# A fused sketch-attention and FFN kernel rewritten: residual algebra, block transposes, column tiles, a scheduled order

## The chip, the cores and the metric

The kernel runs on one core of one Trainium2 chip. Times are device microseconds (us) from launch to end on that core; a run here means one timed execution. Ratios of two kernels are the mean time of one kernel's fast runs over the mean time of the other's fast runs of the same rounds, so they are not quite the ratio of the medians quoted beside them. All comparisons are between runs of state fast, except where a slow one is named.

Engines: PE is the matmul engine (TensorE), DVE the vector engine, ACT the scalar engine (tanh and copies), POOL a second vector engine that is hardly used here, SP the queue that issues most DMAs.

## The reference, cut to what matters

```python
B, H, S, D, r = 4, 4, 1088, 32, 8         # q, k, v: (B, H, S, D) float32; S1, S2: (r, D)
def phi(x):                               # 64 features: outer product of two 8-vectors
    a = S1 @ x;  b = S2 @ x
    return outer(a, b)
kv  = sum_s phi(k_s) v_s^T                # 64 x 32 per batch and head
z   = sum_s phi(k_s)
att = (phi(q) @ kv) / (phi(q) @ z + 1e-6)
x   = att with heads side by side         # (4352, 128)
h   = x @ w_in                            # 128 -> 2048
out = (h - tanh(h)) @ w_out               # 2048 -> 128
```

Two facts of this algebra are used below. First, `(h - tanh(h)) @ w_out = x @ (w_in @ w_out) - tanh(h) @ w_out`. Second, the denominator `phi(q) @ z` is a bilinear form in `S1 q` and `S2 q`, so it can be had from an 8 by 8 matrix per head instead of from a 64-long feature vector.

## The kernel before

Tokens lie on partitions. A chunk of 128 tokens of one batch is transposed on PE, projected, multiplied out, transposed again, and so on. This is the query half of a chunk (waits and buffers cut):

```python
def B_step(b_, c_, qwait, kvzwait):
    tensor.transpose(psT, q_bt[:, c_])                    # token-major -> feature-major
    scalar.copy(T_sb, psT)
    tensor.matmul(psAB, T_sb, psbd)                       # S1 q, S2 q for four heads (float32)
    scalar.copy(ab_sb, psAB)
    vector.tensor_tensor(qp_sb, a[..., None], b[:, None]) # outer product, 256 columns
    for hp in range(2): tensor.transpose(bank_q, qp_sb)   # 2 x 128x128
    scalar.copy(qpT_sb, bank_q)
    for hp in range(2): tensor.matmul(psND, qpT_sb, kvzp_sb)   # numerator and denominator
    vector.tensor_scalar(dtmp, den, 1e-6, add)
    vector.reciprocal(rden, dtmp)
    vector.tensor_tensor(xrow, num, rden, mult)
    tensor.transpose(psX, xrow)                           # back to feature-major for the FFN
    scalar.copy(xT_sb, psX)                               # -> bf16
```

The key half (`A_step`) has the first five steps; after nine chunks of a batch `KVZ` runs 18 float32 matmuls (36 records in the trace). The FFN is cut into blocks that are pulled, about two at a time, after each attention step:

```python
def block_task(jb):                                       # 16 per group of up to 512 tokens
    tensor.matmul(psH, w_in_sb[:, jb*128:(jb+1)*128], xtoks)       # waits for the bank: mF
    scalar.activation(t_sb, psH, Tanh)
    vector.tensor_tensor(g_sb[:, jb], psH, t_sb, subtract)         # frees the bank
def layer2_mm_task():
    for jb in range(16): tensor.matmul(psO, w_out_sb[:, jb], g_sb[:, jb], accumulate)
    ...   # copy, four PE transposes back to token-major, four copies, one DMA
```

There are eight PSUM banks (the buffers that matmuls write): three for attention steps, two for query transposes, three in a ring for the FFN. 1088 tokens are padded to nine chunks of 128.

## Time and profile before

| | before |
|---|---|
| time, median of 4 runs | 471.05 us (469.07 to 473.68) |
| traced span | 470.1 us |
| PE busy, ACT busy, DVE busy | 306.1, 158.2, 150.2 us |
| mean granted PE clock in the trace | 0.665 |
| first tanh starts at | 63.4 us |

The first fence is the page of the profile: busy time of each engine (share of the span, number of instructions), two rows of its 40 equal slices (busy tenths of PE, granted PE clock in tenths), and the chain of waits followed back from the last instruction, by engine and by line.

```profile
PE 306.1 (65%) x1032; PEld 171.8 (37%) x1032; DVE 150.2 (32%) x372; ACT 158.2 (34%) x476; POOL 11.9 (3%) x23
...
PE   0585566677665756686666665685567767778674
...
PEclk9999999996555665555555755755555655665965
...
PE 54%; ACT 20%; DVE 14%; issue 8%; POOL 2%; DMA 1%; ACTq 0%; POOLq 0%
PE psm L536 26%; PE psst L536 23%; ACT tanh L536 8%; DVE g L536 5%; PE psq L536 5%; ACT Tsb L536 4%; DVE qp L536 3%; ACT qpT L536 3%; DVE xrow L536 2%; ACT absb L536 2%; DVE rden L536 1%; DVE dtmp L536 1%; ACT hb L536 1%; POOL psbd L536 1%;
```

No engine is near full, and the chain changes hands all the time. The trace in order of time shows why. This is one query chunk; columns are start, duration, engine, operation and tiles, and in brackets how long the engine had been idle and what ended the wait.

```profile
108.72 0.42 DVE L536 TENSOR_TENSOR qp<-absb 128x256 f32<-128x256 f32 x1 [0.82 <-ACT absb L536]
...
109.20 0.44 PE L536 MATMUL psq<-ident,qp 128*128 128x128 f32 x2 [0.76 <-DVE qp L536]
109.67 0.37 ACT L536 COPY qpT<-psq 128x256 f32<-128x256 f32 x1 [0.99 <-PE psq L536]
...
110.10 0.89 PE L536 MATMUL psst<-kvzp,qpT 128*128 128x66 f32 x4 [0.46 <-ACT qpT L536]
111.02 0.16 DVE L536 TENSOR_SCALAR dtmp<-psst 128x4 f32<-128x4 f32 x1 [1.88 <-PE psst L536]
111.22 0.18 DVE L536 RECIPROCAL rden<-dtmp 128x4 f32<-128x4 f32 x1
111.43 0.29 DVE L536 TENSOR_TENSOR xrow<-psst,rden 128x128 f32<-128x128 f32 x1
...
111.78 0.47 PE L536 MATMUL psst<-ident,xrow 128*128 128x128 f32 x1 [0.79 <-DVE xrow L536]
...
112.29 0.27 ACT L536 CAST xT<-psst 128x128 bf16<-128x128 f32 x1 [2.25 <-PE psst L536]
...
112.33 7.92 PE L536 MATMUL psm<-vbt,wbt 128*128 128x66 f32 x36
```

Each step starts when the one before it ends, on another engine. From one numerator to the next it is 7 to 10 us in 26 of the 35 steps from chunk to chunk, and 11.5 to 17.7 us in the other nine. The last line is the float32 kv chain of the batch.

The second half of the story is PE's clock. The next fence is the listing by windows: the stretch, its length, then busy us (and number of instructions) of PE, weight loads, DVE, ACT, POOL, then the granted clock, the DMA share and GB/s.

```profile
core 0: us, PE busy (x) PEld busy (x) DVE busy (x) ACT busy (x) POOL busy (x), PEclk, DMA share, GB/s
114.00:116.00 2.00, 2.00 (x12) 2.00 (x11) 0.00 (x0) 0.00 (x0) 0.00 (x0) 0.50 0.89 177
...
432.00:434.00 2.00, 2.00 (x6) 0.73 (x5) 0.00 (x0) 0.00 (x0) 0.00 (x0) 0.50 0.00 0
434.00:436.00 2.00, 2.00 (x9) 0.81 (x8) 0.00 (x0) 0.00 (x0) 0.00 (x0) 0.84 0.00 0
...
442.00:444.00 2.00, 1.33 (x4) 0.29 (x3) 2.00 (x4) 1.97 (x4) 0.00 (x0) 1.00 0.00 0
446.00:448.00 2.00, 1.79 (x3) 0.29 (x3) 1.96 (x4) 1.79 (x3) 0.00 (x0) 0.50 0.00 0
```

At 431.3 us sixteen w_out matmuls begin back to back. 3.4 us later the clock goes from 0.50 to 1.00. All eight rises in this trace fall in such a chain, 2.6 to 6.0 us after its start. While FFN blocks are then paced by DVE (one 512-column matmul per 0.60 us), the clock stays up to 445 us and falls back. The kv chain at 112.3 us is dense in the record, and the clock stays at 0.50 (window 114 to 116). So PE runs at half clock most of the time; whether its waits are the reason is tested below (before_nl1_warm). The clock row of the page shows 9 in its first slices, but the trace has no clock record before 103.6 us; the kv matmuls of batch 0 at 26.6 us take the same 7.92 us as those at 112.3 us, where the record says 0.50. The mean of 0.665 counts that stretch as full; at 0.50 there it would be about 0.55, an estimate.

### The profile page before, as it was taken

The numbers are of one execution on the slowest core, as the hardware profiler recorded it, in microseconds if no ns is written. First come the engines' busy times: TensorE is split into PE (matmuls) and PEld (weight loads), VectorE is DVE, ScalarE is ACT, GpSimd is POOL, SyncE is SP. The second block draws the span as 40 slices with busy tenths as digits, with TensorE's granted clock in tenths as the row PEclk, the third lists the DMA queues.
The fourth block names the chain that finished last, engine by engine and source line by source line (L and its number), as shares of the span: only waits on it lengthen the run. The fifth ranks groups of instructions, "written<-read, shape, count | busy, mean of one in ns | idle before, by whom it ended". The sixth has DMA issues, their size and how long they took to land.

```text
span 470.1 us, 3569 instructions
## 1 busy us (share of the span) xinstructions
PE 306.1 (65%) x1032; PEld 171.8 (37%) x1032; DVE 150.2 (32%) x372; ACT 158.2 (34%) x476; POOL 11.9 (3%) x23
## 2 busy tenths in 40 slices
PE   0585566677665756686666665685567767778674
PEld 0373333336433334474332332373432232231222
DVE  0211233411245223211453155103244235256623
ACT  2412233411244223212342344113234225355733
POOL 9100000000000000000000000000000000000000
PEclk9999999996555665555555755755555655665965
DMA  7760000002400024002000300030000000000000
GB/s 203 111 102 2 0 0 1 0 0 53 71 1 1 0 51 64 1 1 42 12 0 0 61 5 0 1 57 1 0 15 0 0 25 1 0 27 0 22 0 26
DMA packets 59443, 11.26 MB, mean 24 GB/s; under 512 B 54432, under 2 KB 58784, under 8 KB 59296
## 3 DMA queue, kind: packets, MB, share of 16 engines
q1 hardware_dynamic: 58496, 8.92, 10.9%
q10 hardware_dynamic: 672, 2.10, 1.4%
q8 instruction: 9, 0.15, 0.1%
q0 software_dynamic: 256, 0.01, 0.1%
q14 instruction: 10, 0.08, 0.1%
HBM read 8.79 MB, written 2.23 MB: 23 GB/s over the span
## 4 chain that ended last, share of the span: by engine, by line
PE 54%; ACT 20%; DVE 14%; issue 8%; POOL 2%; DMA 1%; ACTq 0%; POOLq 0%
PE psm L536 26%; PE psst L536 23%; ACT tanh L536 8%; DVE g L536 5%; PE psq L536 5%; ACT Tsb L536 4%; DVE qp L536 3%; ACT qpT L536 3%; DVE xrow L536 2%; ACT absb L536 2%; DVE rden L536 1%; DVE dtmp L536 1%; ACT hb L536 1%; POOL psbd L536 1%; ACT outsb L536 1%
## 5 line engine op out<-in xcount | busy, mean ns | idle before, releaser
L536 DVE TENSOR_TENSOR g<-psm,tanh 128x512 bf16<-128x512 f32 (+1 forms) x192 | 97.2, 553 | 84.0 <-ACT tanh L536 82.1
L536 ACT ACTIVATE tanh<-psm 128x512 bf16<-128x512 f32 (+1 forms) x192 | 85.9, 491 | 16.4 <-PE psm L536 15.8
L536 PE MATMUL psm<-xT,w_in 128*128 128x512 bf16 (+1 forms) x192 | 81.5, 499 | 13.2 <-DVE g L536 12.3
L536 PE MATMUL psst<-psbd,Tsb 128*128 128x64 f32 x144 | 47.7, 433 | 42.4 <-ACT Tsb L536 39.4
L536 PEld LDWEIGHTS psst<-psbd,Tsb 128*128 128x128 f32 x144 | 34.6, 298 | 73.6 <-ACT Tsb L536 70.4
L536 PE MATMUL psm<-g,w_out 128*128 128x512 bf16 (+1 forms) x192 | 53.5, 463 | 11.4 <-DVE g L536 9.8
L536 PE MATMUL psst<-kvzp,qpT 128*128 128x66 f32 x144 | 38.8, 422 | 16.7 <-ACT qpT L536 16.7
L536 DVE TENSOR_TENSOR wbt<-absb 128x256 f32<-128x256 f32 x36 | 15.3, 425 | 90.0 <-ACT absb L536 90.0
L536 PEld LDWEIGHTS psm<-xT,w_in 128*128 128x128 bf16 x192 | 26.7, 145 | 45.8 <-DVE g L536 36.9
L536 PEld LDWEIGHTS psst<-kvzp,qpT 128*128 128x128 f32 x144 | 32.0, 309 | 30.5 <-ACT qpT L536 30.5
L536 PE MATMUL psq<-ident,qp 128*128 128x128 f32 x72 | 23.8, 432 | 27.5 <-DVE qp L536 27.5
L536 ACT CAST xT<-psst 128x128 bf16<-128x128 f32 x36 | 9.6, 266 | 87.7 <-PE psst L536 87.7
L536 PEld LDWEIGHTS psm<-g,w_out 128*128 128x128 bf16 x192 | 22.9, 136 | 41.4 <-issue 34.7
L536 PE MATMUL psst<-ident,xrow 128*128 128x128 f32 x36 | 17.1, 474 | 28.6 <-DVE xrow L536 28.6
L536 ACT COPY absb<-psst 128x64 f32<-128x64 f32 x72 | 15.3, 213 | 55.3 <-PE psst L536 55.3
L536 DVE TENSOR_TENSOR qp<-absb 128x256 f32<-128x256 f32 x36 | 15.3, 425 | 54.0 <-ACT absb L536 54.0
L536 PE MATMUL psm<-vbt,wbt 128*128 128x66 f32 x144 | 31.6, 422 | 1.0 <-issue 0.9
L536 DVE TENSOR_SCALAR dtmp<-psst 128x4 f32<-128x4 f32 x36 | 5.8, 162 | 82.6 <-PE psst L536 82.6
L536 PEld LDWEIGHTS psm<-vbt,wbt 128*128 128x128 f32 x144 | 31.0, 332 | 1.6 <-issue 1.3
L536 ACT COPY qpT<-psq 128x256 f32<-128x256 f32 x36 | 13.4, 372 | 43.7 <-PE psq L536 43.7
L536 ACT COPY hb<-psm 128x512 f32<-128x512 f32 (+1 forms) x12 | 5.8, 480 | 59.3 <-PE psm L536 59.3
L536 PE MATMUL psst<-ident,kbt 128*128 128x128 f32 x36 | 14.9, 415 | 11.6 <-DMA kbt<-in_k_dram 11.6
(28 smaller groups left out, 129.1 us busy)
## 6 DMA issues: line engine op xcount, KB each, us to landing
kbt<-in_k_dram SPq DMA_DIRECT2D x32, 64.0 KB, 2.5
vbt<-in_v_dram SPq DMA_DIRECT2D x32, 64.0 KB, 2.5
qbt<-in_q_dram SPq DMA_DIRECT2D x32, 64.0 KB, 2.4
out_dram<-outsb SPq DMA_DIRECT2D x8, 256.0 KB, 2.4
w_in_f<-in_moe_w_in_dram ACTq DMA_DIRECT2D x1, 1024.0 KB, 5.1
psbd<-in_S_dram POOLq DMA_DIRECT2D x8, 1.0 KB, 2.6
kbt<-in_k_dram SPq DMA_DIRECT2D x4, 32.0 KB, 2.3
vbt<-in_v_dram SPq DMA_DIRECT2D x4, 32.0 KB, 2.3
```

Source lines behind the costliest of these rows:

```text
L536: ins = getattr(eng_obj, od.method)(*od.args, **od.kw)
```

## The change

The intent is to take work off the token-major path and off DVE, and to make every engine's order overlap-friendly. Five things change together.

```diff
-op("vector", "tensor_tensor", out=g_sb[gs][:, jb, 0:T], in0=psH, in1=t_sb[hs][:, 0:T], op=ALU.subtract)
-... 16 matmuls of g_sb with w_out_sb
+P.add("scalar", ... e.activation(out=th.ap, in_=hv.ap, func=AF.Tanh, scale=-1.0))        # -tanh(h)
+seq = [("t", j) for j in range(NJB)]
+seq[8:8] = [("c", wch), ("c", wcl)]      # x @ (w_in @ w_out), as bf16 high part and bf16 low part
+... 18 matmuls into one bank; w_in @ w_out itself: 16 transposes and 16 matmuls, once
```

```diff
-op("tensor", "transpose", out=psT, in_=k_bt[slot][:, c_, :, :], identity=ident)   # per 128 tokens
-op("scalar", "copy", T_sb[p], psT)
+src = k[b].rearrange("h (t c) d -> (h t) (c d)", c=NC)       # 34 blocks of 32 tokens, no padding
+P.add("vector", lambda e, n: e.transpose(kTa.ap[:, :], kLa.ap[:, :]))   # 32x32 blocks, 576 columns
```

```diff
-op("tensor", "matmul", psAB, T_sb[p], psbd)
+for g in range(4):                       # four column tiles, 32 output partitions each
+    e.matmul(pa.ap[g * 32:(g + 1) * 32, 0:288], sab.ap[:, x, :], t_.ap[:, c0:c0 + 288])
```

The kv products (four tiles of 32 columns) and the numerators (two of 64) use column tiles too, and the numerator comes out feature-major, so `xrow`, its transpose and the `hb` transposes are gone: the output leaves through a DVE block transpose and DMAs with 128-byte rows. The denominator comes from a third projection of q (`sc`), so q's `a` is divided before the outer product.

```diff
-task_q / drain_tasks(rate): FFN blocks slipped in after attention steps
+_Prog.schedule(): a list scheduler with a cost and a key per operation picks each engine's order
+_Prog.sync(): one counting semaphore per engine, only the waits that are needed
```

## The prediction

> **What bounds the kernel now.** Latency, not an engine. The page's first part has PE busy 65%, ACT 34%, DVE 32% of 470 us; the chain of waits is PE 54%, ACT 20%, DVE 14%, issue 8%. In the timeline each 128-token chunk walks through about ten short steps (transpose, copy, projection, copy, outer product, transpose, copy, numerator, three DVE steps, transpose, cast) that wait for one another: 7 to 10 us from one numerator to the next, 36 chunks, FFN blocks slipped in between. And PE runs mostly at half clock: the listing by windows gives a granted clock of 0.50 for most stretches after 100 us. In a w_out chain matmuls start every 0.43 us at first and every 0.21 us once the clock rises (around 435 us); it falls back within about 10 us when PE is only 40% busy. The dense float32 kv chain (36 records, 7.9 us) never raised it.
>
> **What the change does.** It removes 192 DVE subtractions g (97 us busy), the PE transposes of k, q, xrow and hb with their ACT copies, and the padding. It adds two bf16 matmuls per group (x by the high and low part of w_in@w_out), 32 small weight transposes and products, DVE block transposes, and a static order built for overlap.
>
> **Costs after (estimates from before's durations).**
> - ACT: 512-wide tanhs start 0.484 us apart back to back (two in 1.08 us, one 0.596): 128 of them 62 us, 16 of 256 about 4, copies about 15. Sum 82 us.
> - DVE: about 1.04 ns per element (128x512 against 128x128 g) plus a fixed part: about 60 us.
> - PE, FFN: 272 matmuls of 512 and 34 of 256: 62 us at full clock, 123 us at half.
> - PE, attention: 80 projections of 288 columns, 144 kv products, 36 small ones, 72 transposes, 24 numerators, all float32. If column tiles overlap as the Trainium skill ("TensorE: Matmul & The Clock Gate", Part 3) says, about 37 us at full clock, 75 at half; if they run one after another, 40 us more. No trace here shows tiles yet.
>
> So PE (about 100 us at full clock) becomes the bound, just above ACT. All of g goes, but most of it lay off the chain; the gain is the broken latency chain plus a PE dense enough to be clocked up. The same page's Part 1 says sustained activity frees the clock after about 3.4 us; before's trace agrees (0.43 to 0.21 us after about 4 us of dense chain).
>
> **Sum.** Prologue to the first tanh (63 us in before): loads, k side, kv, q side: about 26 us. Then 62 us of FFN and three batches of attention, 28 us, at nearly full clock: 90 us. Tail 4 us. That is 120 us; 18 us more for stretches at half clock, drains where the array's tiling changes, imperfect tile overlap. Predicted 138 us, range 114 to 178.
>
> Chances: faster by over 2% 0.985, within 2% 0.01, slower 0.005.
>
> **What would show it.** PE busy over 80% of the span and leading the chain of waits; ACT 60 to 75%; DVE 40 to 55%, never leading; granted clock near 1.0 from about 30 us on; first tanh at 22 to 32 us; last groups paced by tanh at about 0.49 us; a four-tile projection group in 0.6 us at full clock (1.2 at half).
>
> **What would make it wrong.** If the clock stays at half because float32 work does not count as activity, PE needs about 180 us after the prologue and the time nears 200. If tiles serialize, about 155. If DVE transposes cost twice an ordinary element, DVE adds 25 us and may delay attention. If the fixed order and real durations disagree, ACT starves.

## The result

| | before | after |
|---|---|---|
| time, median of 4 runs | 471.05 us (469.07 to 473.68) | 137.44 us (136.85 to 138.05) |
| ratio | | 0.292, 95% interval 0.2905 to 0.2935 |
| traced span | 470.1 us | 135.4 us |
| mean granted PE clock | 0.665 | 0.973 |
| first tanh starts at | 63.4 us | 31.3 us |

The page of the kernel after, the same lines as shown of before:

```profile
PE 118.0 (87%) x982; PEld 54.8 (40%) x996; DVE 64.9 (48%) x152; ACT 89.4 (66%) x180; POOL 2.4 (2%) x22
...
PE   0477977598989999999999999999999999989970
...
PEclk9999986869999999999999999999999999999999
...
PE 75%; ACT 11%; DVE 6%; DMA 2%; issue 2%; ACTq 0%
PE pso L619 19%; PE psh L607 19%; ACT th L610 11%; PE psa L551 7%; PE psa L541 7%; PE psa L500 5%; PE psa L421 5%; PE pskv L443 4%; PE pskv L453 3%; PE pso L623 3%; DMA s_86<-in_S_dram 2%; PE pskv L468 1%; PE psa L579 1%; DVE ot L628 1%; PE pskv L470 1%
```

PE is busy 87% of the span and leads the chain with 75%; DVE is at 48%, ACT at 66%. The clock row is full from about 30 us on; the first record of the clock is at 15.6 us, and the 9s before it, like the mean of 0.973, count the time without a record as full. Three groups of instructions answer to the FFN (line, engine, operation, tiles, shapes, count, then busy us and mean ns of one, then idle time before and what ended it):

```profile
L610 ACT ACTIVATE th<-psh 128x512 bf16<-128x512 f32 x128 | 67.2, 614 | 19.0 <-PE psh L607 17.3 <-PE psa L421 0.9 <-PE psa L541 0.3
L607 PE MATMUL psh<-xT,wi 128*128 128x512 bf16 x121 | 44.9, 380 | 1.2 <-ACT th L610 0.8 <-issue 0.2
L619 PE MATMUL pso<-th,wo 128*128 128x512 bf16 x122 | 42.3, 381 | 0.8 <-ACT th L610 0.7
```

A few matmul records are missing (121 and 122 of 128). The mean of 380 ns of a 512-column matmul is the duration that the trace models for each one, with its pipeline. Where two FFN matmuls follow each other after 32 us, the second starts 216 ns after the first (median of 220 neighbours, worked out from the start times). The skill's page "Perfetto Trace Analysis" (opening note) warns that matmul busy time is a bad metric for this reason; the experiments below test PE's load by taking work away instead of by reading busy time.

The column tiles, in order of time, PE only:

```profile
29.73 0.44 PE L421 MATMUL psa<-kTa,sab 128*32 128x288 f32 x2
29.74 0.44 PE L421 MATMUL psa<-kTb,sab 128*32 128x288 f32 x2
29.99 0.41 PE L421 MATMUL psa<-kTa,sab 128*32 128x288 f32 x2
30.01 0.41 PE L421 MATMUL psa<-kTb,sab 128*32 128x288 f32 x2
```

Each float32 matmul is two records. Four tiles (two of kTa, two of kTb) start within 0.02 us of one another; the second records of all four start 0.25 us later. Eight records, 288 columns each, take about 0.5 us.

The whole execution in four stretches:

```profile
core 0: us, PE busy (x) PEld busy (x) DVE busy (x) ACT busy (x) POOL busy (x), PEclk, DMA share, GB/s
0.00:31.20 31.20, 20.74 (x208) 11.25 (x210) 16.27 (x40) 10.42 (x17) 2.40 (x22) 0.89 0.93 247
31.20:113.90 82.70, 80.27 (x688) 36.41 (x699) 46.72 (x110) 61.98 (x122) 0.00 (x0) 1.00 0.16 32
113.90:131.00 17.10, 16.68 (x87) 7.02 (x86) 1.43 (x2) 16.96 (x41) 0.00 (x0) 1.00 0.25 38
131.00:135.50 4.50, 0.34 (x2) 0.10 (x1) 0.45 (x1) 0.00 (x0) 0.00 (x0) 0.95 0.30 45
```

From 31.2 to 113.9 us PE is busy 97% and ACT 75%. In the last 17 us no attention is left and ACT is busy 99%, with tanhs back to back; PE is recorded busy 98% there. So there are three stages: a prologue that FFN work does not overlap, a stretch where PE is the fullest engine, and a short end where ACT is full too.

### The profile page after: what moved, and what is told of

The parts are those of the page before. It is cut to its first block, busy times and chain, and to the rows that moved or that the text cites. A ratio compares the mean times of both kernels' runs of the same rounds, so it can differ in the third digit from the quotient of the medians.

```text
span 135.4 us, 2508 instructions
## 1 busy us (share of the span) xinstructions
PE 118.0 (87%) x982; PEld 54.8 (40%) x996; DVE 64.9 (48%) x152; ACT 89.4 (66%) x180; POOL 2.4 (2%) x22
## 4 chain that ended last, share of the span: by engine, by line
PE 75%; ACT 11%; DVE 6%; DMA 2%; issue 2%; ACTq 0%
PE pso L619 19%; PE psh L607 19%; ACT th L610 11%; PE psa L551 7%; PE psa L541 7%; PE psa L500 5%; PE psa L421 5%; PE pskv L443 4%; PE pskv L453 3%; PE pso L623 3%; DMA s_86<-in_S_dram 2%; PE pskv L468 1%; PE psa L579 1%; DVE ot L628 1%; PE pskv L470 1%
## 5 line engine op out<-in xcount | busy, mean ns | idle before, releaser
L610 ACT ACTIVATE th<-psh 128x512 bf16<-128x512 f32 (+1 forms) x144 | 71.7, 592 | 19.0 <-PE psh L607 17.3
L607 PE MATMUL psh<-xT,wi 128*128 128x512 bf16 (+1 forms) x137 | 49.0, 368 | 1.2 <-ACT th L610 0.8
L619 PE MATMUL pso<-th,wo 128*128 128x512 bf16 (+1 forms) x138 | 45.5, 368 | 0.8 <-ACT th L610 0.7
L607 PEld LDWEIGHTS psh<-xT,wi 128*128 128x128 bf16 x144 | 13.9, 97 | 19.4 <-ACT th L610 9.6
L619 PEld LDWEIGHTS pso<-th,wo 128*128 128x128 bf16 x144 | 13.5, 99 | 19.1 <-issue 4.8
L541 PE MATMUL psa<-ident,qp 128*128 128x128 f32 (+1 forms) x72 | 11.7, 289 | 2.5 <-DVE qp L530 2.3
L541 PEld LDWEIGHTS psa<-ident,qp 128*128 128x128 f32 (+1 forms) x72 | 9.0, 147 | 5.9 <-DVE qp L530 2.7
L530 DVE TENSOR_TENSOR qp<-ap,abq 128x768 f32<-128x768 f32 x12 | 11.1, 940 | 0.0
L432 DVE TENSOR_TENSOR w<-abk 128x768 f32<-128x768 f32 x12 | 10.8, 952 | 0.1
L551 PE MATMUL psa<-qpT,kvb 128*64 128x384 f32 (+1 forms) x48 | 10.0, 526 | 0.0
```

Source lines behind the costliest of these rows:

```text
L432: P.add("vector", lambda e, n, p=p, wv=wv: e.tensor_tensor(out=wv.ap.rearrange("p (x i j) -> p x i j", i=8, j=8), in0=ab.ap[:, 0, p * 96:( ...
L530: P.add("vector", lambda e, n, sl=sl, aq=aq, qp=qp, nx=nx: e.tensor_tensor(out=qp.ap[:, 0:nx * 64].rearrange("p (x i j) -> p x i j", i=8, ...
L541: P.add("tensor", lambda e, n, bi=bi, kk=kk, tp=tp, hp=hp, qp=qp: e.transpose(tp.ap[:, bi * 128:bi * 128 + kk], qp.ap[0:kk, bi * 256 + hp ...
L551: i = e.matmul(nm.ap[hp * 64:(hp + 1) * 64, 0:ncol], kvb.ap[:, hp, :], qts[hp].ap[:, 0:ncol], start=True, stop=True)
L607: P.add("tensor", lambda e, n, jb=jb, hv=hv: e.matmul(hv.ap[:, 0:n_], wi[jb // 4].ap[:, (jb % 4) * 128:(jb % 4 + 1) * 128], xt, start=True ...
L610: P.add("scalar", lambda e, n, hv=hv, th=th: e.activation(out=th.ap[:, 0:n_], in_=hv.ap[:, 0:n_], func=AF.Tanh, scale=-1.0), r=[hv], w=[th ...
```

## The experiments

The main theory: the time after is a prologue, in part at half clock, plus the PE work that follows at full clock, with ACT close behind; the overlap comes from the order, and both the algebra and the column tiles are needed to hold DVE and PE at that level. Rivals: tanh on ACT paces the kernel; the removed work alone is the gain and order or tiles are details; the clock alone explains most of it. Eleven kernels were run. The experiments on the kernel after go through the same scheduler, so an edit can shift the static order a little; the control that follows is always the kernel after itself at 137.44 us and ratio 0.292. It was not timed again in the rounds of the experiments; the kernel before was, at medians of 470.69 to 470.75 us against its 471.05.

### half_tanh: half the tanhs, all the matmuls

```diff
-            hv, th = _Val(bank_h), _Val(th_p)
+            hv = _Val(bank_h)
+            if jb % 2 == 0:
+                th = _Val(th_p)
...
+            if jb % 2:
+                continue                 # no activation; the odd block reuses the even block's th
```

> Wrong result on purpose: odd FFN blocks skip their tanh and reuse the even block's; every matmul stays. ACT loses 64 x 0.484 + 8 x 0.27 = 33 us. Theory (PE is the bound after the prologue): little changes, 131 to 138 us against 137.4; a few us may go because the last groups ran at 0.49 us a tanh against 0.43 us a matmul pair. Rival (tanh on ACT paces the kernel): 103 to 115 us.

Measured: 134.65 us median of 4 runs (134.22 to 135.21), ratio 0.2862; result wrong. 33 us of tanh leave ACT and the time falls by 2.8 us. In the stretches before and after the last attention:

```profile
30.90:110.00 79.10, 77.13 (x677) 35.86 (x688) 43.00 (x103) 39.26 (x75) 0.00 (x0) 1.00 0.16 33
110.00:128.00 18.00, 17.95 (x97) 8.97 (x96) 2.15 (x3) 11.54 (x23) 0.00 (x0) 1.00 0.23 37
```

ACT drops to 50% and 64% busy, PE stays at 98 to 100%. ACT does not pace the kernel as a whole. About 2 of the 2.8 us come from the end: from the last attention matmul to the last tanh it is 19.0 us here and 21.0 us in the kernel after.

### half_wo: half of w_out's matmuls, all tanhs

```diff
-        seq = [("t", j) for j in range(NJB)]
-        seq[8:8] = [("c", wch), ("c", wcl)]
+        seq = [("t", j) for j in range(0, NJB, 2)]
+        seq[4:4] = [("c", wch), ("c", wcl)]
```

> Wrong result on purpose: the eight odd w_out matmuls of each group are left out; every tanh stays. PE loses 64 x 0.216 + 8 x 0.11 = 14.7 us. Theory (PE is the bound): 137.4 - 14.7 = 122.7, between 120 and 128 us, ACT now nearly as busy as PE. Rival (ACT paces): 134 to 138 us.

Measured: 129.60 us median of 4 runs (129.24 to 130.47), ratio 0.276; result wrong. The time falls by 7.8 of the 14.7 us that were taken off PE, above the stated range of 120 to 128. PE work counts, so the rival (134 or more) falls; but only half of it came back.

```profile
30.60:90.00 59.40, 57.75 (x557) 25.56 (x564) 37.24 (x88) 47.36 (x93) 0.00 (x0) 1.00 0.19 38
90.00:123.40 33.40, 31.06 (x148) 11.02 (x150) 10.76 (x26) 30.74 (x69) 0.00 (x0) 1.00 0.21 32
```

From 90 us on ACT is busy 92%, with most of its 512-column tanhs 0.48 us apart, back to back: ACT has become a limit for the last 33 us instead of the last 17. (PE's 93% there is modelled busy time, which does not show its slack.) The theory is refined by this: PE is the bound only with ACT a short way behind, about 8 us.

### bf16_num: a smaller PE load with a correct result

```diff
-    qp_p = pool("qp", 4, [128, 3 * 256])
-    qpT_p = pool("qpT", 4, [128, 384])
-    kvb_p = pool("kvb", 2, [128, 2, 64])
+    qp_p = pool("qp", 4, [128, 3 * 256], BF16)     # and transposes with a bf16 identity
+    qpT_p = pool("qpT", 4, [128, 384], BF16)
+    kvb_p = pool("kvb", 2, [128, 2, 64], BF16)
```

> The outer product of q, its transposes and the numerator matmuls go from float32 to bf16 (x is rounded to bf16 right after anyway); nothing else. PE after the first tanh loses about 10 us of the 15.4 that these two groups took there. Theory (PE is the bound while attention still runs, ACT close behind, as the run with half of w_out's matmuls showed by giving back 7.8 of 14.7 us): 129 to 134 us. Rival (PE is dense only because it waits): 136 to 138.

Measured: correct, 131.55 us median of 4 runs (131.09 to 132.09), ratio 0.2794. Worked out from start to next start after the first tanh, the query transposes went from 8.3 to 4.8 us and the numerators from 7.1 to 2.8 us. That is 7.8 us less PE work (about 10 had been expected) and 5.9 us less time, within the stated range.

### sub_on_dve: the residual algebra undone

```diff
-                out=th.ap[:, 0:n_], in_=hv.ap[:, 0:n_], func=AF.Tanh, scale=-1.0)
+                out=th.ap[:, 0:n_], in_=hv.ap[:, 0:n_], func=AF.Tanh)
+            P.add("vector", ... e.tensor_tensor(out=g.ap, in0=hv.ap, in1=th.ap, op=ALU.subtract))
-        seq[8:8] = [("c", wch), ("c", wcl)]          # and no w_in @ w_out product
```

> The algebra is undone and all else kept: g = h - tanh(h) on DVE, no w_in@w_out product, 18 FFN matmuls fewer, the order made anew by the same scheduler. DVE gains 128 x 0.685 + 16 x 0.42 = 94 us on its 65. Theory (the algebra is what keeps DVE off the bound): DVE leads, 168 to 190 us. Rival (overlap and clock alone made the gain, the subtraction lay off the chain): at most 145 us.

Measured: correct, 170.74 us median of 2 runs, ratio 0.3628. (The kernel's 24 tanh buffers became 6, with 24 for g.) Two lines of its page:

```profile
PE 128.2 (76%) x932; PEld 47.4 (28%) x946; DVE 142.0 (84%) x285; ACT 99.1 (59%) x187; POOL 2.4 (1%) x22
...
DVE 52%; PE 31%; ACT 8%; issue 3%; DMA 2%; ACTq 0%; DVEq 0%
```

DVE rises from 64.9 to 142.0 us busy (77 us more; the scheduler also moved copies from DVE to ACT, which rises from 89.4 to 99.1) and is now the fullest engine and leads the chain with 52%. In before the same subtraction lay mostly off the chain (5% of it); here it costs 33 us, because the rest no longer hides it. The rival (at most 145 us) falls.

### untiled_proj: projections without column tiles

```diff
-    i = e.matmul(pa.ap[g * 32:(g + 1) * 32, 0:288], sab.ap[:, x, :], t_.ap[:, c0:c0 + 288], start=True, stop=True)
+    i = e.matmul(pa.ap[:, 0:288], sabm[x].ap[:, g * 128:(g + 1) * 128], t_.ap[:, c0:c0 + 288],
+                 start=(g == 0), stop=(g == 3))       # sabm: zero but for the 32 columns of group g
```

> The 20 projection groups lose their column tiles: masked 128-column weights, four float32 matmuls that accumulate one after another in place of four side by side; result unchanged. Theory (tiles overlap and PE is the bound): a group goes from about 0.5 to about 2 us at full clock, 15 groups x 1.5 = 22 us after the prologue and 8 to 15 us in it: 160 to 180 us. Rival (tiles do not matter, there is slack on PE): at most 142 us.

Measured: correct, 156.70 us median of 2 runs, ratio 0.333: slower by 19.3 us, a little under the stated range and far above the rival's 142. One group without tiles, then one group with tiles in the kernel after:

```profile
49.86 0.38 PE L618 MATMUL psh<-xT,wi 128*128 128x512 bf16 x1
50.08 2.10 PE L510 MATMUL psa<-qT,sc 128*128 128x288 f32 x8
52.02 0.38 PE L630 MATMUL pso<-th,wo 128*128 128x512 bf16 x1
```

```profile
73.57 0.44 PE L421 MATMUL psa<-kTa,sab 128*32 128x288 f32 x2
73.59 0.44 PE L421 MATMUL psa<-kTb,sab 128*32 128x288 f32 x2
73.84 0.41 PE L421 MATMUL psa<-kTa,sab 128*32 128x288 f32 x2
73.85 0.41 PE L421 MATMUL psa<-kTb,sab 128*32 128x288 f32 x2
74.20 0.61 PE L619 MATMUL pso<-th,wo 128*128 128x512 bf16 x2
```

Without tiles it is 1.94 us to the next matmul, with tiles 0.63. Twelve such groups come after the first tanh, about 16 us more PE work, and that stretch grew by 13.8 us. The prologue grew by only 5.7 us (first tanh at 36.9), less than the 8 to 15 expected: with the long untiled chain, which starts at 7.1 us, the clock was full at 11.4 us instead of 29.2. That led to the next run.

### warm46: fillers in PE's early gaps

```diff
+    wd = _Val(bank_o)                                # the output bank, not yet in use
+    for _ in range(46):
+        P.add("tensor", lambda e, n: e.matmul(wd.ap[:, :], wz.ap[:, 0:128], wz.ap[:, :], start=True, stop=True),
+              r=[wz], w=[wd], key=1e9, cost=217)     # lowest priority: fills gaps only
```

> 46 bf16 matmuls on a constant tile into the still unused output bank fill PE's gaps before the first FFN matmul; nothing else changes in value. Theory (the 31 us before the first tanh are long because PE's steps there run at half clock, 20.6 us of PE work in that time): granted clock 1.0 from about 8 us on, first tanh at 25 to 29 us in place of 31.3, total 131 to 135 us. Rival (loads and DVE steps set the prologue): first tanh at 30.5 us or later, total 136 us or more.

Measured: correct, 134.63 us median of 4 runs (133.77 to 134.70), ratio 0.285. The clock is full from 7.1 us on, the first tanh is at 28.2 us instead of 31.3, and the end moves by the same 3 us. So half clock in the prologue cost at least 3 us: the fillers themselves delayed the first real matmul from 4.45 to 7.32 us.

### program_order: the same operations in the order in which they are written

```diff
-                for o in ready:
+                for o in [min(ready, key=lambda o: o.at)]:     # at: place in the program
```

> The same instructions, waits and buffers, but every engine takes them in the order in which the program lists them (all four batches of attention, then the nine FFN groups, in each group 16 w_in blocks and then 18 accumulating matmuls), in place of the list-scheduled order. Theory (the order is what overlaps attention with tanh and keeps PE dense): attention about 31 us for batch 0 and 15 to 20 us for each other, then 8.5 groups of 16 x 0.484 us tanh and 18 x 0.216 us matmuls that no longer overlap, about 11.7 us each: 175 to 205 us, PE idle over 25%. Rival (removed work alone made the gain, the order is a detail): at most 150 us.

Measured: 227.85 us median of 2 runs (225.93 and 229.78), correct, with the profiled run slow. So it was run again:

> program_order again, because its profiled run was of state slow: fast runs at 224 to 230 us, first tanh near 128 us, 11 us from one FFN group to the next.

Measured: 226.72 us median of 3 runs (226.33 to 228.65), profiled run of state fast, ratio 0.4826. Listing by windows, first the attention, then the FFN:

```profile
0.00:127.00 127.00, 81.68 (x692) 40.62 (x693) 64.01 (x141) 19.38 (x39) 2.63 (x22) 0.62 0.24 70
127.00:221.00 94.00, 82.81 (x296) 28.43 (x295) 5.73 (x8) 68.00 (x144) 0.00 (x0) 0.97 0.15 23
```

This was over the 175 to 205 us first expected. The FFN half is as computed: 11.06 us from one group to the next, 16 tanhs (7.94 us) and then 18 accumulating matmuls during which ACT waits 3.11 us. The attention half was underrated: the key projections of the four batches begin at 8.0, 39.4, 68.5 and 97.7 us, so the later batches take about 29 us each, not 15 to 20. Between 44.5 and 112.8 us the clock stood at 0.50, and PE was busy for about 19 of each 29 us; how much of the excess is due to the clock was not tested. Against this one order the scheduled one is worth 89 us with the same instructions (two copies moved from DVE to ACT): it overlaps attention with tanh, and PE's clock stays up. How the 89 us divide between the two was not tested, and an order that interleaves by hand might lose less.

### before_nl1 and before_nl1_warm: what the clock alone is worth in the kernel before

```diff
-    NS, NL, NH = 3, 2, 3
+    NS, NL, NH = 3, 1, 3                 # before_nl1: one query bank fewer
+def keep(n):                             # before_nl1_warm adds this, into the freed bank,
+    for _ in range(n):                   # behind each attention step of PE, n = 1 to 3
+        op("tensor", "matmul", bank_d[:, :], wz[:, 0:128], wz[:, :])
```

> Control for the next: the kernel before with one query bank in place of two, which frees a PSUM bank. 465 to 482 us: the chunks follow one another so closely that the second bank is hardly used.

> As before_nl1, with one to three bf16 matmuls on a constant tile behind each of PE's attention steps, into the freed bank, to keep PE dense while it waits. Theory (half clock is a consequence of the gaps, and a good part of the time before): granted clock over 0.9, 380 to 440 us. Rival (the chain of waits alone sets the time, clock matters little): 465 us or more. Either way far from 137: if it stays above 350, the clock alone does not explain the gain.

Measured: before_nl1 471.47 us median of 2 runs (ratio 1.0001, interval 0.9897 to 1.0105), so the freed bank costs nothing. before_nl1_warm 409.78 us median of 2 runs, ratio 0.8693; both correct. Its clock row:

```profile
PEclk9999999999999999999999999999998977757676
```

The clock stays full for most of the span (mean 0.928, first record at 21.4 us) and the time falls 13%, although 396 useless matmuls were added. A kv chain, the same 36 records, now starts its matmuls over 3.93 us instead of the 7.50 of before_nl1. So the half clock followed from how PE's time was filled, and was worth at least 13%. The fillers close gaps and are bf16 matmuls of 512 columns at once; which of the two the clock answers to is not separated here. The kv chain, dense in the record, did not raise the clock in before, so gaps alone do not explain it. The clock is not the main part: with the clock nearly full, the chain of short steps still takes 410 us. The rival falls.

### prologue and all_gc: towards a faster version

prologue is warm46 with 34 fillers, fewer of them at the front, q of batch 0 loaded ahead of the weights, and the small products for the 8 by 8 matrix of the denominator (the gram products) put in after the first third of kv. all_gc adds bf16_num and another cut of the groups (with 24 fillers):

```diff
-GCOLS = [512] * 8 + [256]
+GCOLS = [384] + [512] * 7 + [384]
-            load(key - 12000, lambda lo=lo, hi=hi: qL.ap[:, lo:hi], ...)
+            load(key - (12000 if b else 13000), lambda lo=lo, hi=hi: qL.ap[:, lo:hi], ...)
```

> As warm46, with 34 filler matmuls and fewer of them ahead of the first real one, q of batch 0 loaded ahead of the weights, and the small gram products put in after the first third of kv. Theory (the prologue is a chain of real steps at full clock now, so each step that leaves it counts): first tanh at 24 to 27 us in place of 28.2, total 130 to 134. If loads set it: no change from 134.6.

> bf16_num and prologue together, and groups of 384, seven of 512, 384 columns, so that the first FFN group needs one third of batch 0's queries. Theory (prologue, then PE with ACT right behind it, add up): first tanh at 22 to 26 us, 121 to 128 us.

prologue measured 134.92 us median of 4 runs (133.51 to 135.37), ratio 0.286: no gain over warm46, a miss. The first tanh did come at 24.1 us instead of 28.2, but the last attention matmul moved by only 0.9 us. Eight of the 34 fillers had been scheduled behind the first tanh, where PE is the bound, and took 1.8 us there; they also hold the output bank. The other 1.4 us are spread over the new order.

all_gc measured 121.14 us median of 4 runs (120.18 to 122.75), correct. The run of 122.75 us is slow; the fast ones are 120.18, 120.56 and 121.73. Ratio of fast runs 0.2573 against 0.292: 12% faster than the kernel after, and the fastest version here.

```profile
0.00:21.20 21.20, 18.15 (x212) 9.11 (x212) 14.19 (x37) 9.62 (x17) 2.87 (x23) 1.00 0.99 262
21.20:95.00 73.80, 73.49 (x699) 33.29 (x699) 50.24 (x121) 56.65 (x117) 0.00 (x0) 1.00 0.30 66
95.00:113.30 18.30, 18.00 (x87) 7.15 (x86) 1.93 (x3) 18.04 (x40) 0.00 (x0) 1.00 0.20 30
```

The prologue is 21.2 us, then PE is busy 99.6%, then PE and ACT are both busy over 98% for 18 us. The first tanh, at 21.2 us, is a little earlier than the 22 to 26 expected. bf16_num gained 5.9 us and prologue 2.5; the fast median of all_gc is 16.9 us below the kernel after, so about half of its gain came with the group cut or from the three together. The group cut was not measured on its own, and why it gains so much stays open.

## Why the prediction was right

The predicted 138.0 us stand against 137.44, and the three-stage account held. The terms, one by one:

| term | predicted | in the trace |
|---|---|---|
| up to the first tanh | 26 | 31.3 |
| FFN on PE after it | 62 | 64.6 |
| attention on PE after it | 28 | 32.3 |
| PE waiting in that stretch | in the 18 | 2.8 |
| after the last tanh | 4 | 4.4 |
| half clock, drains, imperfect overlap | 18 | spread over the rows above |
| sum | 138 | 135.4 span, 137.4 timed |

FFN and attention are start-to-next-start times on PE from the first tanh to the end of the last, less PE's idle time, which is the waiting row. Against the 120 us of the named terms the span has 15.4 us more, and 2.0 us of the timed 137.4 lie outside the span. So the near-exact total is in part luck: it rests on the allowance of 18 us, which was an estimate without a trace behind it.

- **The bound.** Right: PE 87% busy and leading the chain with 75%, ACT at 66%, DVE at 48%, all inside the stated bands. half_tanh, half_wo and bf16_num show it by taking work away. "Just above ACT" was right in kind: half_wo got only half of its PE saving back before ACT took over.
- **The clock.** Right: full from 29.2 us on, also in the stretches with attention, where FFN matmuls are mixed in; in program_order attention alone ran at 0.50 from 44.5 to 112.8 us. Part of what the skill's page "TensorE: Matmul & The Clock Gate" (Part 1) says, that sustained activity releases the clock, is seen here in both kernels (in before 3.4 us after the w_out chain at 431.3 us began). That filling PE's time raises it in before, and is worth 13%, is shown by before_nl1_warm; that the gaps as such held it down is not.
- **Column tiles.** Right: four float32 tiles start within 0.02 us of one another, as Part 3 of the same page says of tiles, and a group takes 0.5 to 0.6 us against the 0.6 predicted and 1.94 untiled.
- **Drains at tiling changes.** The page "TensorEngine Tiling (Array Packing)" (§ Key Properties) says that changing the tiling mode drains the engine. The trace agrees that such a change costs time, and gives a size: an FFN matmul of 512 columns is followed after 216 ns (median) by another FFN matmul or by an untiled transpose (8 cases), but after 309 ns by a tiled one (27 cases: 24 with column tiles, 3 of 32 rows). In untiled_proj the same float32 projections follow after 216 ns (10 cases), so it is the tiling and not the type. That is 93 ns on the way in, 2.5 us in all, which here is counted in the FFN row.
- **The subtraction.** The prediction said that all of g goes but that most of it lay off the chain. True for before, and sub_on_dve adds what it did not say: in the new kernel the same subtraction would cost 33 us.
- **The prologue.** Mis-sized, 26 us against 31.3. About 3 us of the difference is half clock in it (warm46). The rest was not taken apart further.
- **Attention after the prologue.** I counted three batches, 28 us, and the trace has 32.3. The amount of work was about right: a third of batch 0's queries comes after the first tanh (6 of the 60 query transposes and 4 of the 40 numerator records there, about 1.6 us), and batch 1's key projections, about 1.3 us, come before it. So the cost was underrated by about 4 us; which operations cost more was not taken apart.
- **ACT and DVE.** Predicted 82 and 60 us, measured 89.4 and 64.9. The 384-column copies take 0.48 to 0.49 us each on ACT.

What stays open: the DVE block transposes had no run of their own (they and the PE transposes that they replace need different layouts throughout), so their share of the gain is only argued. Nor was any one of the five changes tried alone in the kernel before; the runs show what the kernel after loses without each of three of them (algebra, projection tiles, order). The page "VectorE: DVE Perf Modes" (§ The three transpose paths) says that DVE transposes 32x32 blocks only; that is why the token layout changed with them. In the trace 576 columns of float32 take 764 ns and 512 take 681, and all of them together 27 us of DVE.

## What to carry to other kernels

When no engine is full and the chain passes from engine to engine, look at the order first: here the same instructions took 227 us in written order and 137 in a scheduled one. Gaps on PE may be paid twice, once as waiting and once as half clock in the work around them (13% of the kernel before came back when they were filled); count the work at both clocks before choosing what to cut. To find the bound of a dense kernel, take work away from one engine at a time and see how much time comes back: half of the PE work removed here came back, because the next engine was 8 us behind.

## What the Trainium skill lacked or had wrong

- "TensorE: Matmul & The Clock Gate", Part 1, lets the clock rise after a busy window of about 3.4 us. In before, float32 kv matmuls that kept PE busy for 7.9 us with no gap (128 columns of weights loaded per 66 columns of data) never raised it; bf16 chains of 512 columns raised it 2.6 to 6.0 us after their start (eight chains), and untiled float32 chains of 288 columns raised it by 11.4 us. The page names no measure of activity that would tell these apart.
- The same part lets the clock fall after an idle window, and tells of a kernel whose clock swings because PE idles briefly and often, without a size for such gaps. In before it fell at 445 us without an idle window, and this gives a size: PE was starting a 512-column matmul of 216 ns every 0.60 us for the 5 us in front of it.
- The same page, § Back-to-back issue gap, gives about 131 ns a matmul for 512 columns in a stream of weight loads and matmuls, and 216 ns for a matmul in isolation. Here a stream of such pairs ran at 216 ns (median of 220 neighbours), never near 131; it fits the 215.7 ns that Part 1 gives for matmuls back to back.
- "TensorEngine Tiling (Array Packing)" gives no size for the drain at a change of tiling, and no figure for float32: the runs show 93 ns on the way into a tile, and 0.63 us against 1.94 us for four 32-column float32 tiles of 288 columns with and without tiling.
